# Five bf16 casts of the W_out combinations on GpSimd, with a re-annealed order of steps, in a fused cross-covariance attention and GELU MLP kernel

## The chip, the cores and the metric

The kernel runs on one core of one Trainium2 chip. The metric is the device time of one launch in microseconds (us); less is better. A core has five engines that work in parallel, each through its own instructions in order: TensorE (PE, matmuls from SBUF into PSUM), VectorE (DVE), ScalarE (ACT), GpSimd (POOL) and SyncE (SP, used here for DMAs). An engine that needs another's result waits for a semaphore. PSUM has eight banks, which this kernel hands out by name.

## What is computed

```python
qn = q / (norm(q, axis=1) + 1e-6)            # q, k, v: [4, 6080, 256]
kn = k / (norm(k, axis=1) + 1e-6)
a  = softmax(kn.transpose(0, 2, 1) @ qn / tau)   # [4, 256, 256]
x  = (v @ a).reshape(24320, 256)
h  = x @ w_in                                # [24320, 2048]
g  = 0.5 * h * (1 + tanh(sqrt(2/pi) * (h + 0.044715 * h**3)))
out = g @ w_out                              # [24320, 256]
```

Inputs and output are fp32; the kernel multiplies in bf16 with fp32 sums.

## The kernel before, in words

**The work.** For each of the four batches the kernel forms the 256x256 Gram matrix of K and Q and the squared norms, makes the softmax matrix `a` of them, and folds it into the first weight: `aw = a @ w_in`, 256x2048, in bf16. The MLP then is gelu(v @ aw) @ w_out. It goes over 25 blocks of tokens (mostly 1024; the 6080 tokens of a batch end in one of 960, the last batch in one of 448 and one of 512). Block n, half f of the hidden units and half t of the tokens give the activations `g`.

**Seven products in place of eight.** Both matmuls of a block are cut into 2x2 quarters and done as a Winograd form of Strassen's scheme: seven products m1 to m7 (first matmul) and M1 to M7 (second) instead of eight, at the price of sums. Sums of the V halves are made by `sums_v` (L568, step `vs`), of the aw halves by `sums_w` (L558, `SW`), of the activations by `token_sum` (L695, steps T1 to T4). The second matmul's other operand is eight combinations of the quarters of W_out, the tile `wcomb` (each 128 x 1024 bf16): A11, A12, A21, A22 are plain casts of a quarter, S1 to S4 are sums and differences. M1 reads A11, M2 A12, M3 S4, M4 A22, M5 S1, M6 S2, M7 S3; A21 is read only in the last block. In block 0 and in parts of block 1 the first matmul is done plainly (steps `g`, with `G` for the GELU).

**W_out's preparation** (L651 to L688). `load_wout` brings W_out as fp32 into `wst`, in two halves, through GpSimd's DMA queue. `prep_wout` has ten steps of one instruction each, all 128x1024: pA11 casts A11; pF0 makes wf0 = A21 - A22 in fp32, pS1 casts it to S1; pF1 makes wf1 = A11 - wf0, pS2 casts it to S2; pS4 and pS3 are differences that write bf16; pA12, pNA (A22) and pA21 cast quarters. `wst` shares its buffer with block 1's second half of `g`, so that half's GELUs can only write when all readers of `wst` are done. It happens once, in the first 65 us, beside block 0.

**What sets the order.** Nothing is scheduled by the compiler. The string `ORDER` (from L1008) lists 4030 steps; `run` (L918) takes them one by one and issues each step's instructions on their engines, so every engine's queue is in the order of this string. A word is `step.arguments@bank:block` (or `:batch`); `@f` names the PSUM bank. The string was annealed against a planner's costs. The steps that the text below names: `g`, `m1` to `m7`, `M1` to `M7`, `aw`, `vp` (V transposes on PE) and `row` (Gram rows) are PE's; `ac` (aw out of PSUM), `vc` (V out of PSUM), `SW`, `vs`, `T1` to `T4`, `ksq`/`qsq` (squares of K and Q; some on ACT) and `f1` to `f3` (their folds) are mostly VectorE's; `G`, `wG*`, `wcq`, `wy5`, `cq`, `y5` are ScalarE's.

**GpSimd's queue.** The steps `lq`, `lk` (`load_one`, L96) and `lv` (`cast_v`, L443) issue the DMAs of Q, K and V for later use, with a cast to bf16 under way. Each is made to wait for the matmul issued last before it (the `GATE`), so that loads are spread over time. T3 of blocks 1 to 22 is a DMA that accumulates (L709). All of these pass through GpSimd in order, one behind the other. Apart from them it does little: two fills and a `pow` of 128x4 per batch (L298).

Of the kernel before, what the change touches and what calls it, by code (L numbers as in the profile page):

```python
# [11 lines left out]
AF = mybir.ActivationFunctionType  # L12
# [4 lines left out]
def kernel(  # L17
# [648 lines left out]
    def prep_wout(what):  # L666
        if what == "pA11":
            nc.vector.tensor_copy(wc(A11), w_half(0, 0))
        if what == "pF0":
            WF.append(yout.tile([128, 32, 32], FP32, tag="ot", name="wf0"))  # L670
            nc.vector.tensor_sub(WF[0], w_half(1, 0), w_half(1, 1))
        if what == "pS1":
            nc.vector.tensor_copy(wc(S1), WF[0])
        if what == "pF1":
            WF.append(yout.tile([128, 32, 32], FP32, tag="ot", name="wf1"))
            nc.vector.tensor_sub(WF[1], w_half(0, 0), WF[0])
        if what == "pS4":
            nc.vector.tensor_sub(wc(S4), w_half(0, 1), WF[1])
        if what == "pS2":
            nc.vector.tensor_copy(wc(S2), WF[1])  # L680
        if what == "pA12":
            nc.scalar.activation(wc(A12), w_half(0, 1), AF.Copy)
        if what == "pNA":
            nc.scalar.activation(wc(A22), w_half(1, 1), AF.Copy)
        if what == "pA21":
            nc.scalar.activation(wc(A21), w_half(1, 0), AF.Copy)
        if what == "pS3":
            nc.vector.tensor_sub(wc(S3), w_half(1, 0), w_half(0, 0))  # L688
# [320 lines left out]
g.1_0@f:0 aw.2@g:0 g.0_0@e:0 aw.3@a:0 ac.2:0 g.2_0@b:0 ac.3:0 vp.1@z:0 G.0_0:0 g.6_0@c:0 aw.4@d:0  # L1009
vc.1_0:0 vc.1_1:0 g.4_0@g:0 aw.5@e:0 aw.7@a:0 ac.4:0 ac.5:0 ac.7:0 lk.0:1 SW.0:0 G.6_0:0 g.5_0@c:0  # L1010
pS3:0 g.5_1@d:0 aw.6@e:0 ac.6:0 G.2_0:0 G.1_0:0 lq.0:1 g.0_1@b:0 G.4_0:0 G.5_0:0 G.5_1:0 G.0_1:0
g.7_0@f:0 g.11_1@g:0 g.10_1@c:0 g.7_1@a:0 pA21:0 g.1_1@d:0 G.11_1:0 vp.0@z:1 g.8_0@b:0 pA11:0
G.7_1:0 G.7_0:0 G.1_1:0 G.10_1:0 g.12_0@g:0 SW.1:0 g.4_1@a:0 g.2_1@e:0 g.6_1@f:0 g.13_1@d:0 G.12_0:0
g.9_1@c:0 vc.0_0:1 pF0:0 lv.1:1 G.2_1:0 G.6_1:0 G.4_1:0 vc.0_1:1 G.13_1:0 g.11_0@g:0 g.15_0@e:0
g.10_0@f:0 g.3_0@a:0 g.3_1@d:0 G.11_0:0 g.0_0@g:1 G.8_0:0 G.15_0:0 G.3_0:0 lq.1:1 g.12_1@b:0 pF1:0
lt.1:1 pS1:0 pS2:0 T1.1:0 G.0_0:1 G.3_1:0 G.9_1:0 g.8_1@e:0 G.10_0:0 g.11_0@a:1 G.8_1:0 G.12_1:0
g.4_0@g:1 pS4:0 g.3_0@d:1 T1.0:0 ksq.0:1 qsq.0:1 g.13_0@c:0 g.9_0@f:0 g.15_1@e:0 g.14_1@b:0 G.4_0:1
G.9_0:0 G.3_0:1 G.14_1:0 G.15_1:0 g.14_0@g:0 row.0_2@z:1 G.13_0:0 lk.1:1 g.7_0@f:1 m1.1@d:1
row.0_4:1 row.0_0:1 M1.0@b:0 T2.1:0 f1.0:1 G.7_0:1 pNA:0 g.2_0@e:1 lk.2:1 pA12:0 M5.1@c:0 M5.0:0
wcq.1@f:1 G.2_0:1 G.11_0:1 G.14_0:0 M1.1:0 lv.0:2 g.8_0@e:1 G.8_0:1 row.0_3:1 y5:0 row.0_5:1 m2.1:1  # L1020
g.15_0@a:1 g.10_1@g:1 vs:1 lq.2:1 m5.1@e:1 g.10_0@c:1 wGp.1:1 G.15_0:1 wy5.1:1 f2.0:1 T2.0:0
g.15_1@f:1 m6.1:1 m5.6@a:1 g.11_1@e:1 G.10_0:1 f3.0:1 wap.1@c:1 row.0_1:1 T3.1:0 row.1_0:1 row.1_4:1
lv.1:2 G.15_1:1 G.11_1:1 G.10_1:1 m1.5@f:1 m7.1:1 g.2_1@e:1 m3.1:1 row.1_2:1 cq@g:0 row.1_1:1
row.1_3:1 row.1_5:1 wGs.1:1 wax.1:1 wy5.6:1 m5.5@c:1 m4.1:1 T4.1:0 gc:1 lq.3:1 M6.1:0 T3.0:0
sp.0@z:1 M6.0:0 M2.0:0 wy5.5:1 wGr.1:1 qsq.1:1 ksq.1:1 ap@a:0 M2.1:0 G.2_1:1 wcq.5@c:1 g.0_1@d:1
# [369 lines left out]
```

## Time and profile before

| | before |
|---|---|
| time, median of 3 runs | 677.4 us (677.34 to 677.78) |
| the profiled execution's own time | 677.52 us |
| its span, first to last instruction | 675.7 us |
| granted TensorE clock | 0.999 |
| DMA | 101.70 MB, mean 151 GB/s |

The profile's totals give each engine's busy time as a share of the span. The view of waits names, for each engine and line, whom it waited for, with the total, the number and the longest. The view by windows gives the busy time of the engines in each stretch, then the granted clock, the DMA share and GB/s. A timeline row is start, length, engine, line, operation and tiles; where several instructions are merged, the length runs from the first's start to the last's end, and `x` counts them. Lengths of neighbours on one engine overlap a little; the distance from start to start is what an instruction costs its engine.

### The profile page before, as it was taken

The numbers are of one execution on the slowest core, as the hardware profiler recorded it, in microseconds if no ns is written. First come the engines' busy times: TensorE is split into PE (matmuls) and PEld (weight loads), VectorE is DVE, ScalarE is ACT, GpSimd is POOL, SyncE is SP. The second block draws the span as 40 slices with busy tenths as digits, with TensorE's granted clock in tenths as the row PEclk, the third lists the DMA queues.
The fourth block names the chain that finished last, engine by engine and source line by source line (L and its number), as shares of the span: only waits on it lengthen the run. The fifth ranks groups of instructions, "written<-read, shape, count | busy, mean of one in ns | idle before, by whom it ended". The sixth has DMA issues, their size and how long they took to land.

```text
span 675.7 us, 10621 instructions
## 1 busy us (share of the span) xinstructions
PE 659.6 (98%) x3557; PEld 334.3 (49%) x3557; DVE 629.0 (93%) x977; ACT 624.4 (92%) x1201; POOL 113.1 (17%) x177
## 2 busy tenths in 40 slices
PE   3999999999999999999999999999999999999997
PEld 1854454554454454544444445445444444444567
DVE  3688999999999999999999999999999999999994
ACT  4389999999999999999999999999998999999984
POOL 4321121230211211102111111122011011011100
PEclk9999999999999999999999999999999999999999
DMA  9998899999879997868979999697484576457343
GB/s 241 208 263 134 145 171 172 180 154 168 158 153 182 168 178 128 167 103 150 148 147 169 186 149 191 103 172 147 101 156 98 117 152 140 80 122 154 63 95 107
DMA packets 167207, 101.70 MB, mean 151 GB/s; under 512 B 148128, under 2 KB 152352, under 8 KB 166432
## 3 DMA queue, kind: packets, MB, share of 16 engines
q0 software_dynamic: 20688, 62.34, 53.3%
q1 hardware_dynamic: 145264, 37.13, 26.3%
q10 hardware_dynamic: 1200, 1.56, 0.7%
q8 instruction: 28, 0.46, 0.3%
q14 instruction: 27, 0.22, 0.1%
HBM read 78.91 MB, written 36.57 MB: 171 GB/s over the span
## 4 chain that ended last, share of the span: by engine, by line
PE 94%; DMA 4%; DVE 1%; issue 0%; ACT 0%; POOL 0%; DVEq 0%; ACTq 0%; POOLq 0%
PE rb L491 20%; PE p L491 18%; PE q L491 16%; PE r L491 12%; PE m L491 11%; PE h L491 8%; PE G L205 5%; DMA qk_g1b<-in_k_dram 3%; PE awp L379 2%; DMA qk_g1a<-in_q_dram 1%; PE o L491 1%; PE ss L186 0%; PE ss L267 0%; PE rk L321 0%; DVE sq L160 0%
## 5 line engine op out<-in xcount | busy, mean ns | idle before, releaser
L491 PEld LDWEIGHTS <-wcomb 128*128 128x128 bf16 x1344 | 130.6, 98 | 144.6 <-issue 1.2
L641 ACT ACTIVATE g<-q 128x512 bf16<-128x512 f32 (+1 forms) x306 | 182.1, 621 | 4.4 <-PE q L491 3.8
L491 PE MATMUL rb<-tv,sw 128*128 128x512 bf16 (+3 forms) x334 | 117.0, 368 | 0.0
L632 DVE TENSOR_TENSOR q<-rb,yw 128x512 f32<-128x512 f32 (+2 forms) x160 | 108.6, 685 | 8.2 <-ACT g L549 2.3
L715 DVE TENSOR_TENSOR t<-g,t 128x2048 bf16<-128x2048 bf16 (+2 forms) x96 | 112.3, 1177 | 0.0
L635 DVE TENSOR_TENSOR xw<-rb,yw 128x512 f32<-128x512 f32 (+2 forms) x160 | 107.4, 675 | 3.8 <-PE rb L491 2.3
L491 PEld LDWEIGHTS <-aw 128*128 128x128 bf16 x757 | 73.4, 98 | 73.9 <-issue 1.0
L641 ACT ACTIVATE g<-xw 128x512 bf16<-128x512 f32 (+1 forms) x153 | 99.3, 652 | 1.2 <-DVE xw L635 1.2
L623 ACT ACTIVATE q<-rb 128x512 f32<-128x512 f32 (+2 forms) x160 | 96.8, 611 | 3.3 <-PE rb L491 1.7
L491 PEld LDWEIGHTS <-sw 128*128 128x128 bf16 x668 | 65.0, 98 | 64.4 <-issue 1.1
L641 ACT ACTIVATE g<-rb 128x512 bf16<-128x512 f32 (+1 forms) x153 | 93.5, 617 | 3.3 <-PE rb L491 3.0
L491 PE MATMUL r<-g,wcomb 128*128 128x512 bf16 (+2 forms) x384 | 95.1, 372 | 0.0
L491 PE MATMUL p<-t,wcomb 128*128 128x512 bf16 (+2 forms) x384 | 95.1, 372 | 0.0
L629 ACT ACTIVATE yw<-m 128x512 f32<-128x512 f32 (+2 forms) x145 | 89.8, 625 | 2.6 <-PE m L491 1.5
L549 ACT ACTIVATE g<-h 128x512 bf16<-128x512 f32 (+1 forms) x124 | 71.9, 647 | 3.8 <-PE h L491 3.7
L709 POOL DMA_DIRECT2D g<-g x44 | 39.5, 942 | 205.7 <-ACT g L641 109.8
L491 PE MATMUL h<-vT,aw 128*128 128x512 bf16 (+1 forms) x256 | 69.7, 378 | 0.3 <-DVE aw L421 0.3
L491 PE MATMUL q<-vT,sw 128*128 128x512 bf16 (+3 forms) x167 | 60.1, 368 | 0.0
L491 PE MATMUL q<-vT,aw 128*128 128x512 bf16 (+3 forms) x167 | 59.6, 368 | 0.0
L491 PE MATMUL rb<-vT,aw 128*128 128x512 bf16 (+3 forms) x167 | 59.4, 368 | 0.0
L491 PE MATMUL m<-tv,sw 128*128 128x512 bf16 (+3 forms) x167 | 59.3, 368 | 0.0
L491 PE MATMUL rb<-tv,aw 128*128 128x512 bf16 (+3 forms) x167 | 59.1, 368 | 0.0
(154 smaller groups left out, 876.3 us busy)
## 6 DMA issues: line engine op xcount, KB each, us to landing
out_dram<-ot SPq DMA_DIRECT2D x161, 128.0 KB, 3.4
g<-g POOLq DMA_DIRECT2D x38, 512.0 KB, 5.9
vb<-in_v_dram POOLq DMA_DIRECT2D x38, 256.0 KB, 5.1
k<-in_k_dram POOLq DMA_DIRECT2D x21, 384.0 KB, 6.3
q<-in_q_dram POOLq DMA_DIRECT2D x21, 384.0 KB, 6.7
g<-g POOLq DMA_DIRECT2D x6, 480.0 KB, 6.2
out_dram<-ot SPq DMA_DIRECT2D x24, 120.0 KB, 5.6
wst<-in_moe_w_out_dram POOLq DMA_DIRECT2D x2, 1024.0 KB, 10.0
```

The costliest lines, as they stand in the source:

```text
L205: nc.tensor.matmul(G[b][:, jc, :], lhsT=qt[:np_, r, jc * 128 : jc * 128 + 128], rhs=kt[:np_, r, :], start=first and jc == 0, stop=jc == 1, ...
L379: nc.tensor.matmul(ps, lhsT=ET[b][:, jc, ic * 128 : ic * 128 + 128], rhs=win_bf[:, jc, fs * 512 : fs * 512 + 512], start=jc == 0, stop=jc ...
L491: GATE[0] = nc.tensor.matmul(*a, skip_group_check=True, **kw)
L549: nc.scalar.activation(g_half(n, u // 8)[:, x, u % 8], hp[:, :hc], AF.Gelu_apprx_tanh)
L623: nc.scalar.activation(Q[n, i, 0][:, :w], RB[n, i][:, :w], AF.Copy)
L629: nc.scalar.activation(YW[n, i][:, :w], M5.pop((n, i))[:, :w], AF.Copy)
L632: nc.vector.tensor_add(Q[n, i, 1][:, :w], RB[n, i][:, :w], YW[n, i][:, :w])
L635: nc.vector.tensor_add(XW[n, i][:, :w], RB[n, i][:, :w], YW.pop((n, i))[:, :w])
L641: nc.scalar.activation(g[:, t, k0], x[:, :w], AF.Gelu_apprx_tanh)
L709: nc.gpsimd.dma_start(out=o, in_=quarter(n, 1, 1, h), accum_op=ALU.add)
L715: (nc.vector.tensor_add if add else nc.vector.tensor_sub)(o, a, b)
```

## The change

Five of the ten preparation steps move to GpSimd: S1 and S2 from VectorE, A12, A22 and A21 from ScalarE.

```diff
         if what == "pS1":
-            nc.vector.tensor_copy(wc(S1), WF[0])
+            nc.gpsimd.tensor_copy(wc(S1), WF[0])
...
         if what == "pS2":
-            nc.vector.tensor_copy(wc(S2), WF[1])
+            nc.gpsimd.tensor_copy(wc(S2), WF[1])
         if what == "pA12":
-            nc.scalar.activation(wc(A12), w_half(0, 1), AF.Copy)
+            nc.gpsimd.tensor_copy(wc(A12), w_half(0, 1))
         if what == "pNA":
-            nc.scalar.activation(wc(A22), w_half(1, 1), AF.Copy)
+            nc.gpsimd.tensor_copy(wc(A22), w_half(1, 1))
         if what == "pA21":
-            nc.scalar.activation(wc(A21), w_half(1, 0), AF.Copy)
+            nc.gpsimd.tensor_copy(wc(A21), w_half(1, 0))
```

`ORDER` holds the same 4030 words with the same arguments and blocks. Their places differ in five stretches, each followed by one where they are as before: the first 458 words, words 500 to 823, 1600 to 1798, 2503 to 2698 and 3100 to 3300 (by the old kernel's matmuls about 37 to 116 us, 122 to 170, 290 to 320, 430 to 460 and 522 to 556). Bank letters differ throughout. Part of the new string, from its 44th word on (the old one's order of the same steps can be read in the kernel above):

```
vp.0@z:1 g.4_1@f:0 g.9_1@c:0 lq.0:1 pA21:0 g.7_1@b:0 g.12_0@d:0 g.15_1@g:0 lv.1:1 G.4_1:0 G.9_1:0
G.11_0:0 G.7_1:0 g.10_1@f:0 g.13_1@c:0 G.15_1:0 G.12_0:0 g.8_1@a:0 vc.0_0:1 vc.0_1:1 pA11:0 pF0:0
pA12:0 lq.1:1 pF1:0 pS3:0 SW.1:0 G.13_1:0 pS4:0 G.8_1:0 G.6_1:0 T1.1:0 ksq.0:1 g.11_1@b:0 g.4_0@g:1
g.14_0@d:0 g.12_1@c:0 pNA:0 G.4_0:1 g.10_0@a:0 g.0_1@e:0 G.10_1:0 g.1_1@g:0 g.13_0@f:0 G.12_1:0
qsq.0:1 g.8_0@c:1 G.10_0:0 G.0_1:0 lt.1:1 g.15_0@a:0 g.10_0@e:1 G.14_0:0 G.11_1:0 G.15_0:0 f1.0:1
row.0_5@z:1 f2.0:1 row.0_2:1 g.9_0@d:0 g.2_0@b:1 g.15_0@a:1 row.0_4:1 lk.1:1 G.1_1:0 G.9_0:0 G.15_0:1
M1.1@g:0 g.14_1@d:0 G.2_0:1 G.13_0:0 T1.0:0 G.10_0:1 G.8_0:1 G.14_1:0 pS1:0 g.0_0@a:1 lv.0:2 T2.0:0
f3.0:1 g.7_0@b:1 M1.0:0 G.0_0:1 vs:1 g.3_0@f:1 m1.1@e:1 M5.1@c:0 lq.2:1
...
M5.0:0 row.0_1:1 m5.1@a:1 row.0_0:1 G.7_0:1 G.11_1:1 lv.1:2
...
T3.0:0 cq@c:0 pS2:0
...
```

More of the change, by code (lines that the diff above doesn't have):

```diff
@@ L1008 @@
 ORDER = """
[L1009 to L1025, printed above, removed]
@@ new lines @@
+g.7_0@d:0 g.5_0@e:0 aw.5@b:0 aw.4@c:0 G.7_0:0 G.3_0:0 G.0_0:0 g.6_0@d:0 vc.1_0:0 vc.1_1:0 g.3_1@a:0
+g.2_1@g:0 G.5_0:0 G.6_0:0 G.2_1:0 G.3_1:0 G.1_0:0 aw.6@e:0 g.5_1@d:0 ac.5:0 ac.4:0 ac.6:0 g.8_0@b:0
+g.4_0@c:0 G.4_0:0 SW.0:0 aw.7@g:0 g.11_0@a:0 ac.7:0 g.6_1@e:0 G.8_0:0 G.5_1:0 vp.0@z:1 g.4_1@f:0
+g.9_1@c:0 lq.0:1 pA21:0 g.7_1@b:0 g.12_0@d:0 g.15_1@g:0 lv.1:1 G.4_1:0 G.9_1:0 G.11_0:0 G.7_1:0
+g.10_1@f:0 g.13_1@c:0 G.15_1:0 G.12_0:0 g.8_1@a:0 vc.0_0:1 vc.0_1:1 pA11:0 pF0:0 pA12:0 lq.1:1 pF1:0
+pS3:0 SW.1:0 G.13_1:0 pS4:0 G.8_1:0 G.6_1:0 T1.1:0 ksq.0:1 g.11_1@b:0 g.4_0@g:1 g.14_0@d:0
@@ new lines @@
+g.12_1@c:0 pNA:0 G.4_0:1 g.10_0@a:0 g.0_1@e:0 G.10_1:0 g.1_1@g:0 g.13_0@f:0 G.12_1:0 qsq.0:1
+g.8_0@c:1 G.10_0:0 G.0_1:0 lt.1:1 g.15_0@a:0 g.10_0@e:1 G.14_0:0 G.11_1:0 G.15_0:0 f1.0:1
+row.0_5@z:1 f2.0:1 row.0_2:1 g.9_0@d:0 g.2_0@b:1 g.15_0@a:1 row.0_4:1 lk.1:1 G.1_1:0 G.9_0:0
+G.15_0:1 M1.1@g:0 g.14_1@d:0 G.2_0:1 G.13_0:0 T1.0:0 G.10_0:1 G.8_0:1 G.14_1:0 pS1:0 g.0_0@a:1
+lv.0:2 T2.0:0 f3.0:1 g.7_0@b:1 M1.0:0 G.0_0:1 vs:1 g.3_0@f:1 m1.1@e:1 M5.1@c:0 lq.2:1 G.3_0:1
+wcq.1@d:1 g.10_1@a:1 G.10_1:1 m2.1:1 g.11_1@f:1 M5.0:0 row.0_1:1 m5.1@a:1 row.0_0:1 G.7_0:1 G.11_1:1
@@ new lines @@
+lv.1:2 m6.1:1 y5:0 m1.5@b:1 T3.1:0 m5.5@f:1 row.0_3:1 wy5.1:1 wGp.1:1 T3.0:0 cq@c:0 pS2:0 row.1_0:1
+row.1_1:1 row.1_5:1 row.1_3:1 wap.1@a:1 lk.2:1 T2.1:0 row.1_2:1 row.1_4:1 wcq.5@d:1 wy5.5:1 M2.0:0
+gc:1 m2.5:1 m3.1:1 m7.1:1 sp.0@z:1 wGp.5:1 wGs.1:1 ksq.1:1 wax.1:1 qsq.1:1 g.15_1@f:1 m6.5:1 M6.1:0
+M2.1:0 g.11_0@d:1 wap.5@a:1 lt.1:2 f1.1:1 c11:0 f2.1:1 m3.5:1 m7.5:1 M6.0:0 G.11_0:1 G.15_1:1
+wGx.1:1 lt.0:2 g.2_1@d:1 g.0_1@g:1 lq.3:1 G.2_1:1 m4.1:1 sa.0:1 ap@f:0 wax.5:1 M3.1:0 G.0_1:1 f3.1:1
+m5.6@d:1 m1.6@g:1 m4.5:1 sp.1@z:1 M7.1:0 wGx.5:1 lk.3:1 wGr.1:1 wcq.6@e:1 wy5.6:1 T4.1:0 T4.0:0
@@ new lines @@
+c11:2 wGs.3:3 wGx.2:3 m2.4:3 row.4_0:1 m5.4@b:3 m7.3:3 m6.4:3 m1.5@e:3 c22:1 wGp.4:3 ksq.6:1 wax.3:3
+m5.5@a:3 M6.0:2 wy5.4:3 wGr.2:3 wcq.5@b:3 wap.4@d:3 row.4_1:1 wy5.5:3 m4.3:3 m6.5:3 m3.4:3 wGx.3:3
+row.4_2:1 row.4_3:1 m2.5:3 m7.4:3 wGr.3:3 f1.6:1 wGp.5:3 wap.5@a:3 row.5_4:1 wax.4:3 row.5_0:1
+wGs.4:3 m5.6@f:3 f2.6:1 ap@b:2 wGx.4:3 row.4_4:1 m7.5:3 row.5_3:1 row.5_5:1 m4.4:3 wy5.6:3 wGr.4:3
+f3.6:1 m1.6@d:3 m3.5:3 M3.1:2 lt.0:4 wcq.6@f:3 gc:1 sp.6@z:1 wGs.5:3 m5.7@g:3 wax.5:3 sa.6:1 qsq.7:1
@@ new lines @@
+m2.6:3 m6.6:3 ksq.7:1 M7.0:2 M7.1:2 wGp.6:3 wGx.5:3 wap.6@a:3 m3.6:3 lt.1:4 f1.7:1 ax:2 lv.0:5
+m1.7@f:3 m4.5:3 m7.6:3 wGs.6:3 M3.0:2 wcq.7@a:3 m6.7:3 lq.0:2 M4.1:2 wax.6:3 f2.7:1 wy5.7:3
+wap.7@g:3 f3.7:1 m4.6:3 m3.7:3 m2.7:3 m7.7:3 wGx.6:3 wGr.5:3 wGs.7:3 g.8_0@e:3 sp.7@z:1 c12:2
+wax.7:3 sa.7:1 T1.0:3 wGp.7:3 g.0_0@b:4 m1.3@g:4 wGr.6:3 lk.0:2 m4.7:3 G.8_0:3 M4.0:2 row.7_0@z:1
+m1.1@a:4 row.7_1:1 wGr.7:3 wcq.3@d:4 m2.3:4 row.6_4:1 g.0_1@e:4 vs:4 G.0_0:4 wcq.1@f:4 T3.0:3 m6.3:4
+m5.1@b:4 m2.1:4 pow:1 lv.1:5 row.6_5:1 row.7_2:1 m6.1:4 wGp.3:4 wGx.7:3 wy5.1:4 T1.1:3 c21:2
@@ new lines @@
+G.0_1:6 m3.5:6 wax.5:6 m6.6:6 wap.6@c:6 wGs.5:6 m1.4@d:6 M6.0:5 wcq.4@g:6 wGx.5:6 m4.5:6 m3.6:6
+m7.6:6 row.0_0:2 m5.7@b:6 row.1_5:2 T4.0:5 wGs.6:6 wGr.5:6 wax.6:6 m2.4:6 row.0_2:2 wy5.7:6 m5.4@c:6
+m6.4:6 lk.4:2 ap@f:5 m4.6:6 wy5.4:6 m1.7@b:6 wGp.4:6 wcq.7@c:6 lv.0:9 M3.1:5 wGr.6:6 M3.0:5 m6.7:6
+gc:2 T4.1:5 wGx.6:6 wap.4@g:6 m2.7:6 m3.4:6 m7.4:6 wGp.7:6 M7.0:5 wap.7@e:6 wax.4:6 m7.7:6 wGx.4:6
+m3.7:6 m4.4:6 wGr.4:6 wGs.4:6 c12:5 M7.1:5 m1.4@c:7 wGs.7:6 wax.7:6 m4.7:6 g.8_0@f:7 ax:5 g.8_1@d:7
@@ new lines @@
+G.8_1:12 T1.1:11 m1.4@e:12 m4.3:12 wGx.3:12 row.1_2:3 wGs.1:12 wGr.3:12 wcq.4@c:12 wax.1:12
+M5.0@a:11 SW.1:2 T3.1:11 M5.1:11 m1.2@b:12 m2.4:12 wGx.1:12 y5:11 wGp.4:12 row.1_1:3 T2.1:11
+row.1_5:3 wcq.2@d:12 m4.1:12 m6.4:12 m5.4@a:12 M1.1@c:11 wy5.4:12 wy5.2:12 wGr.1:12 m2.2:12 T2.0:11
+lq.2:3 lk.2:3 m6.2:12 M1.0:11 m1.5@a:12 wap.4@g:12 m3.4:12 wap.2@f:12 m7.4:12 row.0_4:3 m3.2:12
+m7.2:12 wGp.2:12 ksq.1:3 cq@d:11 wax.4:12 wGs.4:12 wcq.5@g:12 M2.1:11 T4.1:11 wGs.2:12 wGx.4:12
+m2.5:12 m4.4:12 wGr.4:12 wGp.5:12 m6.5:12 m5.5@f:12 M2.0:11 wax.2:12 c22:10 wy5.5:12 m1.6@e:12
```

643 lines of the change are left out of this document (310 added, 333 removed).

## The prediction, made before the changed kernel was run

> **What bounds the kernel now.** I read the page's totals first, then the list of what TensorE waits for, then stretches of 10 us, then the chain of waits, and last the timelines of VectorE and GpSimd around W_out's preparation.
>
> ```profile
> span 675.7 us, 10621 instructions
> PE 659.6 (98%) x3557; PEld 334.3 (49%) x3557; DVE 629.0 (93%) x977; ACT 624.4 (92%) x1201; POOL 113.1 (17%) x177
> ...
> PE G L205 <- ACT qk_g1a L131: 10.2, 2, 7.2
> PE ss L261 <- DVE a L243: 1.3, 1, 1.3
> PE h L491 <- DVE aw L421: 0.3, 1, 0.3
> PE q L491 <- DVE q L815: 0.2, 1, 0.2
> ...
> 40.00:50.00 10.00, 10.00 (x59) 4.97 (x57) 9.58 (x19) 8.88 (x17) 1.09 (x2) 1.00 1.11 312
> 50.00:60.00 10.00, 10.00 (x51) 4.81 (x50) 10.00 (x12) 10.00 (x21) 1.94 (x4) 1.00 0.76 120
> 60.00:70.00 10.00, 10.00 (x60) 5.37 (x58) 7.59 (x12) 9.97 (x20) 2.31 (x5) 1.00 0.92 151
> ...
> 46.84 9.93 PE h L491 x46
> ```
>
> TensorE (PE) is the bound: 98% of the span. The waits that it lists are four lines, 12.0 us together; three of them belong to the head (no Q and K yet, no weights yet), and only the last, 0.2 us, comes after the head. A busy PE could still hide gaps, since one matmul's record overlaps the next. The chain's row at 46.84 shows that there are none there: 46 matmuls of 512 columns in 9.93 us are 0.216 us each, start to start, without a break. Taking every start-to-start interval above that pitch, from the first matmul of the plain steps to the last of the kernel,
>
> ```profile
> 37.53 0.65 PE L491 MATMUL h<-vT,aw 128*128 128x512 bf16 x2 [0.31 <-DVE aw L421]
> ...
> 668.65 3.22 PE L491 MATMUL o<-wcomb,g 128*128 128x256 bf16 x28
> ```
>
> I find about 2.3 us of gaps in all, of which 0.2 lie before 116 us (where W_out is prepared) and about 0.7 in the three later stretches whose steps the change reorders. So there is next to nothing to win: 0.9 us if every gap in the reordered stretches went. There is much to lose, since each us that PE waits is a us of the kernel. The windows from 40 to 60 us say who could make it wait: VectorE (DVE) and ScalarE (ACT) are both at 8.9 to 10.0 of 10.
>
> **The change part by part.** In the built program both versions give PE the same 3554 matmuls with the same 1,532,204 columns, in another order. PE's work therefore is unchanged; only waits can differ. Removed from the two busy engines:
>
> ```profile
> 44.77 1.05 ACT L686 ACTIVATE wcomb<-wst 128x1024 bf16<-128x1024 f32 x1
> 45.72 13.32 ACT L549 ACTIVATE g<-h 128x512 bf16<-128x512 f32 x27
> 58.70 1.26 ACT L684 ACTIVATE wcomb<-wst 128x1024 bf16<-128x1024 f32 x1
> 59.65 1.25 ACT L682 ACTIVATE wcomb<-wst 128x1024 bf16<-128x1024 f32 x1
> ...
> 50.57 1.21 DVE L676 TENSOR_TENSOR wf<-wst,wf 128x1024 f32<-128x1024 f32 x1
> 51.70 0.68 DVE L673 CAST wcomb<-wf 128x1024 bf16<-128x1024 f32 x1
> 52.30 0.68 DVE L680 CAST wcomb<-wf 128x1024 bf16<-128x1024 f32 x1
> 52.90 1.21 DVE L715 TENSOR_TENSOR t<-g 128x2048 bf16<-128x2048 bf16 x1
> 54.04 1.21 DVE L678 TENSOR_TENSOR wcomb<-wst,wf 128x1024 bf16<-128x1024 f32 x1
> 55.17 1.21 DVE L715 TENSOR_TENSOR t<-g 128x2048 bf16<-128x2048 bf16 x1
> 56.31 0.95 DVE L160 TENSOR_TENSOR sq<-k 128x1536 bf16<-128x1536 bf16 x1
> 57.18 0.95 DVE L160 TENSOR_TENSOR sq<-q 128x1536 bf16<-128x1536 bf16 x1
> 58.09 1.23 DVE L715 TENSOR_TENSOR t<-g,t 128x2048 bf16<-128x2048 bf16 x1
> ```
>
> ACT loses 0.95 us each by start-to-start (58.70 to 59.65), 2.85 us in all; VectorE 2 x 0.60 (51.70, 52.30, 52.90), 1.2 us. That relief itself is worth 0, because PE is not waiting there; its worth is only that the new order may call for results sooner.
>
> Added to GpSimd (POOL): five casts, 128x1024 fp32 to bf16. No row shows such a cast on it. The nearest are
>
> ```profile
> 0.24 0.10 POOL L1376 MEMSET const-float32-0.0<- 128x1 f32 x1 [0.24 <-issue]
> 4.65 0.27 POOL masks.py:197 MEMSET ident<- 128x128 f32 x1
> 4.99 0.29 POOL masks.py:199 TENSOR_SCALAR_AFFINE_SELECT ident<-ident 128x128 f32<-128x128 f32 x1
> ```
>
> The same cast on ScalarE, 1.05 us (at 44.77), is my lower end. GpSimd's own slope from 1 to 128 elements is 0.17 us for 127, which over 1024 gives 0.10 + 1.37, about 1.45 us: the upper one. I take the middle, 1.25. The Trainium skill (GPSIMD Engine Reference, section Elementwise — side-by-side cycle accounting) gives 1.8 cycles of 1.2 GHz an element as the best loop; by that estimate a cast is 1.54 us and each term below grows by a quarter. No run here shows it yet.
>
> GpSimd also issues the DMAs of Q, K and V, in order, each held back until a given matmul. A step's time in the new order I get by adding the columns of the matmuls ahead of it at 0.216 us per 512, from 37.5 us (for the old order this puts the first M5 at 59.1). An issue takes 0.53 to 0.55 us and follows its matmul by 0.3 to 0.5:
>
> ```profile
> 43.67 0.53 POOL L103 DMA_DIRECT2D q<-in_q_dram  x1 [1.17 <-PE h L491]
> 50.16 0.53 POOL L447 DMA_DIRECT2D vb<-in_v_dram  x1 [5.95 <-PE h L491]
> ...
> DMA to landing us min/median/max: 4.5/5.0/8.1
> ```
>
> The new queue is then: q1_0 at 48.4, pA21 at 48.9, vb1_1 at 50.2, pA12 at 50.7, q1_1 at 52.0, pNA at 52.5, k1_1 at 57.6, pS1 at 58.1, and later pS2 at 65.2. Three consumers could be late. q1_0 (issued at 43.67 before) lands at 53.4 by the median, at 56.5 at worst; the first gram row wants it at 55.5: cost 0, up to 1.0. S1 is ready at 59.4 for M5.1 at 61.0, S2 at 66.5 for M6.1 at 68.7, A12 and A22 long before use: cost 0. A21 is used in the last block only.
>
> VectorE is where it bites. In the new order its run from the second V transpose (47.3) to block 1's sums_v is, by the pitches above and these two rows,
>
> ```profile
> 60.10 0.68 DVE L573 TENSOR_TENSOR tv<-vT 128x1024 bf16<-128x1024 bf16 x1
> ...
> 61.62 0.42 DVE L181 TENSOR_TENSOR sq<-sq 128x512 bf16<-128x512 bf16 x1
> ```
>
> two copies of about a fold's 0.35 and pA11 at 0.60 (ends 48.7), pF0, pF1, pS3 (52.2), four sums of SW.1 (53.6), pS4, T1.1 (55.9), four squares and folds (58.9), T1.0 (60.1), T2.0, one fold, and sums_v at 1.5 (60.10 to 61.62), which ends at 63.2. m5.1 of block 1 reads sums_v's result at 63.9. So the margin is 0.7 us; T1.0 has 3 us before M5.0 at 62.9. T2.0 and a fold, 1.5 us, now run ahead of sums_v though M6 needs them only at 72.
>
> Does a cast on GpSimd slow VectorE? The trace has one GpSimd instruction that reads SBUF beside VectorE's work, three times:
>
> ```profile
> 138.25 1.65 POOL L298 TENSOR_TENSOR rt<-sv,halves 128x4 f32<-128x4 f32 x1
> 138.34 0.64 DVE L573 TENSOR_TENSOR tv<-vT 128x1024 bf16<-128x1024 bf16 x1
> 309.61 0.68 DVE L635 TENSOR_TENSOR xw<-rb,yw 128x512 f32<-128x512 f32 x1
> 309.78 1.05 POOL L298 TENSOR_TENSOR rt<-sv,halves 128x4 f32<-128x4 f32 x1
> 460.00 1.22 DVE L715 TENSOR_TENSOR t<-g 128x2048 bf16<-128x2048 bf16 x1
> 460.07 2.05 POOL L298 TENSOR_TENSOR rt<-sv,halves 128x4 f32<-128x4 f32 x1
> ```
>
> Beside an instruction with one operand in PSUM (xw) it took 1.05 us; beside one with both inputs in SBUF it took 0.60 longer (that instruction: 0.64) and 1.00 longer (of 1.22). The two engines share something, and GpSimd waited for it. These rows read four elements, so they can't show how long VectorE waits for a 1024-element read. Nearly all of the run from pF0 to sums_v has both inputs in SBUF, so four casts (pA21, pA12, pNA, pS1) meet it. What each takes from VectorE lies between nothing (it gives way, as the rows show) and its whole length. I take half of 1.25, halfway, since no row is nearer to either end: 4 x 0.62 = 2.5 us, less the margin of 0.7: **PE waits 1.8 us at m5.1**. pS2's place is followed by margins of about 1.6: 0. The gaps in the reordered stretches may give 0.2 back.
>
> The sum is +1.6 on the profiled execution's 677.52 (span 675.7 and 1.8 around it); that run lies 0.1 above the median of 677.4, so 679.0.
>
> The Trainium skill (SBUF — State Buffer, section Who interferes with whom) says that VectorE's second pair of ports is GpSimd's only one, that an instruction with two SBUF inputs contends with a GpSimd instruction that reads SBUF, and that whoever comes first holds it to its end. The rt rows agree for GpSimd's waits (0.60 and 1.00); for VectorE's no row does.
>
> **The rivals.**
> *Held for the whole cast.* Four whole casts at 1.05 to 1.45 are 4.2 to 5.8 us, less 0.7: 3.5 to 5.1, so 680.7 to 682.3. For it: VectorE's 10.00 of 10 in the window from 50 on. Against it: a cast that starts where VectorE works from PSUM holds nothing. The State Buffer page of the Trainium skill, above, would have it go this way.
> *GpSimd gives way.* VectorE loses under 0.2 us a cast, the sum stays below the margin of 0.7, and the order's shaved gaps leave 677.2, at most 0.2 us under the median. It decides from a loss of 0.7/4, about 0.2, a cast. For it: in both shared rt rows VectorE's instruction kept its length. This is the case on the other side, not slower.
> *GpSimd starves.* If it gives way to an unbroken run, pS1 comes after 61.0, and PE waits at M5.1 for S1, with the later issues behind it. A wait of one T (1.1) at each of two casts stays inside pS1's room of 1.6 only barely: 678 to 681.
> *Every gap goes.* 677.4 - 0.9 = 676.5; over 0.2% faster (below 676.05) would need gaps outside the reordered stretches too. That the casts don't move is excluded: the built program has all five on GpSimd.
>
> **How the numbers follow.** Held for a part (678.2 to 680.0) 0.36, held whole 0.24, gives way 0.32, starves 0.04, gaps go 0.04. A measurement can tell about 0.2%, 1.35 us, from no change: below 676.05 and above 678.75. Slower: 0.24 + 0.25 of the first case + 0.03 = 0.52; faster 0.03, as the last case mostly stays within; same 0.45. The range from 676.8 to 682.0 leaves out the longest holds and the best of the gaps. The cases that are not slower have their own range, 676.6 to 678.2.
>
> **What would show it.** A row PE m <- DVE tv, or a gap at m5.1 near 64 us, of 1 to 2 us; SBUF-with-SBUF instructions of VectorE between 48 and 64 us longer than 1.23, or spaced wider than 1.14; casts of 1.0 to 2.5 us on GpSimd. If VectorE's rows keep their pitch, the sum is wrong at the hold; if PE waits for wcomb, GpSimd starved; if a gap stands past 120 us, the new order did it and not the casts.

## The result, and the profile after

The changed kernel takes **682.26 us** (median of 20 runs, 681.91 to 682.77), the kernel before 677.77 (20 runs beside them, 677.34 to 683.36). The ratio is 1.0059, 95% interval 1.0049 to 1.0069: slower by 3.3 to 4.7 us. Here and below the ratios are not those of the medians: single executions some us above the rest (before: 680.59 and 683.36) move them, so both are given. The prediction was 679.0, in a range from 676.8 to 682.0; the time lies 0.3 above its upper end and 0.04 inside the rival "held for the whole cast" (680.7 to 682.3). But the kernel before took 0.4 us more here than the 677.4 that the prediction starts from: 677.4 times the ratio is 681.4, inside the range, near its upper end and in the middle of that rival.

The profiled execution after took 682.38 us with a span of 680.6 (before: 677.52 and 675.7). These are its totals, what TensorE waited for after the head, and the two windows from 50 to 70 us (columns as before):

```profile
span 680.6 us, 10605 instructions
PE 661.4 (97%) x3557; PEld 334.4 (49%) x3557; DVE 634.8 (93%) x975; ACT 623.6 (92%) x1198; POOL 120.5 (18%) x182
...
PE h L491 <- ACT g L549: 2.3, 1, 2.3
PE m L491 <- DVE tv L573: 1.0, 1, 1.0
PE q L491 <- DVE q L632: 0.8, 1, 0.8
...
50.00:60.00 10.00, 8.92 (x45) 4.21 (x43) 9.93 (x8) 7.36 (x16) 4.82 (x7) 1.00 0.89 141
60.00:70.00 10.00, 7.83 (x40) 3.76 (x40) 9.83 (x14) 8.18 (x17) 2.29 (x4) 1.00 0.59 98
```

Three waits are new: TensorE waits 2.3 us for a GELU, 1.0 us for block 1's `sums_v` (the place that the prediction named) and 0.8 us for a sum at L632. From 50 to 70 us its busy time falls from 20.00 to 16.75, while VectorE is as good as full (19.76). Counted as in the prediction (start-to-start intervals over the pitch of 0.216 us for 512 columns, records that are missing from the trace left out), TensorE's gaps between 37 and 116 us are 5.25 us where they were 0.24; after 116 us they are 2.3 where they were 2.0. So nearly the whole loss stands beside the preparation of W_out, and the later stretches of the new order gave nothing. Here is why VectorE is late. First GpSimd's timeline of the changed kernel, then VectorE's and ScalarE's:

```profile
48.63 0.53 POOL L103 DMA_DIRECT2D q<-in_q_dram  x1 [7.39 <-PE h L491]
49.16 1.05 POOL L686 CAST wcomb<-wst 128x1024 bf16<-128x1024 f32 x1
50.15 0.53 POOL L447 DMA_DIRECT2D vb<-in_v_dram  x1
50.67 1.05 POOL L682 CAST wcomb<-wst 128x1024 bf16<-128x1024 f32 x1
51.65 0.55 POOL L103 DMA_DIRECT2D q<-in_q_dram  x1
52.20 1.05 POOL L684 CAST wcomb<-wst 128x1024 bf16<-128x1024 f32 x1
57.71 0.53 POOL L103 DMA_DIRECT2D k<-in_k_dram  x1 [4.46 <-PE h L491]
58.23 1.05 POOL L673 CAST wcomb<-wf 128x1024 bf16<-128x1024 f32 x1
...
69.27 1.71 POOL L680 CAST wcomb<-wf 128x1024 bf16<-128x1024 f32 x1
```

```profile
48.78 5.55 DVE L671 TENSOR_TENSOR wf<-wst 128x1024 f32<-128x1024 f32 x1
...
58.11 2.26 DVE L678 TENSOR_TENSOR wcomb<-wst,wf 128x1024 bf16<-128x1024 f32 x1
...
67.34 0.68 DVE L573 TENSOR_TENSOR tv<-vT 128x1024 bf16<-128x1024 bf16 x1
...
68.86 3.19 DVE L715 TENSOR_TENSOR g<-g,g 128x2048 bf16<-128x2048 bf16 x2
71.97 0.69 DVE L632 TENSOR_TENSOR q<-rb,yw 128x512 f32<-128x512 f32 x1
```

```profile
60.53 4.03 ACT L549 ACTIVATE g<-h 128x512 bf16<-128x512 f32 x8 [3.17 <-DVE wcomb L678]
```

The row to read first is pF0 at 48.78: one subtraction of 5.55 us, where it took 1.21. It began 0.38 us *before* the first cast and ended at 54.33, which is 1.08 us after the third cast's end (53.25): about the length of a subtraction. So it did next to nothing through three casts and the two DMA issues between them. pS4 at 58.11 took 2.26 beside S1's cast (+1.05), and the pair of T3 sums at 68.86 took 3.19 beside S2's, where such a pair takes 2.35 (+0.84). VectorE loses 4.34 + 1.05 + 0.84 = 6.2 us.

The lateness shows first where the prediction did not look. `wst` shares its buffer with block 1's second half of `g`; pS4 (L678) is its last reader, and ScalarE's GELU at 60.53 has waited 3.17 us for it. TensorE runs on until no PSUM bank is free and then stands still for 2.42 us from 58.76, 1.12 us from 66.96 (m5.1, for `sums_v`) and 0.93 us from 71.79 (L632).

### The profile page after: what moved, and what is told of

The parts are those of the page before. It is cut to its first block, busy times and chain, and to the rows that moved or that the text cites. A ratio compares the mean times of both kernels' runs of the same rounds, so it can differ in the third digit from the quotient of the medians.

```text
span 680.6 us, 10605 instructions
## 1 busy us (share of the span) xinstructions
PE 661.4 (97%) x3557; PEld 334.4 (49%) x3557; DVE 634.8 (93%) x975; ACT 623.6 (92%) x1198; POOL 120.5 (18%) x182
## 4 chain that ended last, share of the span: by engine, by line
PE 87%; DVE 5%; DMA 4%; ACT 2%; issue 1%; POOL 1%; DVEq 0%; POOLq 0%; ACTq 0%
PE rb L491 19%; PE p L491 17%; PE q L491 15%; PE r L491 11%; PE m L491 10%; PE h L491 6%; PE G L205 4%; DMA qk_g1b<-in_k_dram 3%; PE awp L379 2%; DMA qk_g1a<-in_q_dram 1%; ACT g L641 1%; DVE wf L671 1%; DVE t L715 1%; DMA out_dram<-ot 1%; PE o L491 1%
## 5 line engine op out<-in xcount | busy, mean ns | idle before, releaser
L632 DVE TENSOR_TENSOR q<-rb,yw 128x512 f32<-128x512 f32 (+2 forms) x160 | 108.7, 686 | 5.1 <-PE rb L491 1.1
```

The lines of the kernel that those rows point to most:

```text
L632: nc.vector.tensor_add(Q[n, i, 1][:, :w], RB[n, i][:, :w], YW[n, i][:, :w])
```

## The experiments

The theory behind the first four: the casts' hold on VectorE is the whole loss. The rivals: the new order of steps does it, or ScalarE's share. Each run is compared with the kernel before on the same chip; its median there was 677.51 us for e1 to e4, 677.34 for e5 to e7 and 677.59 for e8. "VectorE held" is what VectorE's instructions between 42 and 72 us took over their usual length, "TensorE's gaps" are those from 37 to 116 us; both are us of the profiled execution.

| kernel | time, us | ratio to before, 95% interval | VectorE held | TensorE's gaps |
|---|---|---|---|---|
| before | 677.77 | | 0 | 0.24 |
| changed | 682.26 | 1.0059 (1.0049 to 1.0069) | 6.2 | 5.25 |
| e1 new order, casts as before | 679.93 | 1.0035 (1.0023 to 1.0048) | 0 | 2.33 |
| e2 old order, casts on GpSimd | 677.91 | 1.0019 (0.9999 to 1.0039) | 4.7 | 1.32 |
| e3 new order, two casts | 679.16 | 1.0030 (1.0019 to 1.0040) | 1.1 | 2.33 |
| e4 new order, three casts | 683.60 | 1.0084 (1.0068 to 1.0099) | 4.2 | 4.47 |
| e5 pS4 earlier | 682.44 | 1.0077 (1.0062 to 1.0092) | 6.4 | 5.58 |
| e6 `sums_v` earlier too | 682.69 | 1.0080 (1.0065 to 1.0095) | 6.4 | 5.47 |
| e7 issues taken out from between | 680.76 | 1.0051 (1.0034 to 1.0068) | 5.1 | 4.11 |
| e8 each cast waits for the last | 680.77 | 1.0046 (1.0029 to 1.0063) | 4.6 | 3.52 |

**e1_order_only: the order alone.** The changed kernel with all five casts back on VectorE and ScalarE.

```diff
-            nc.gpsimd.tensor_copy(wc(S1), WF[0])
+            nc.vector.tensor_copy(wc(S1), WF[0])
...
-            nc.gpsimd.tensor_copy(wc(A12), w_half(0, 1))
+            nc.scalar.activation(wc(A12), w_half(0, 1), AF.Copy)
```

> The new order of steps with all five casts back on VectorE and ScalarE. If the casts on GpSimd cost the time (they stop VectorE: its first subtraction took 5.55 us in place of 1.21), nearly all of the loss of 4.5 us goes: 677.0 to 678.2, no gap of over 0.3 us on PE between 40 and 75 us, the subtraction at 1.21. If the new order costs it (margins annealed too thin), 681 or more, with the gaps at the same steps as in the changed kernel.

Measured: 679.93 us, above what was expected and below what the rival would have. VectorE's subtractions are at 1.22 again and between 40 and 116 us TensorE waits for none of its results, but 1.6 us are gone elsewhere. These are rows of this kernel's list of waits and of ScalarE's timeline:

```profile
PE h L491 <- ACT g L549: 1.3, 2, 0.8
...
51.06 1.13 ACT L682 ACTIVATE wcomb<-wst 128x1024 bf16<-128x1024 f32 x1
...
53.44 1.16 ACT L684 ACTIVATE wcomb<-wst 128x1024 bf16<-128x1024 f32 x1
```

Two casts on ScalarE now stand among GELUs for which TensorE waits (gaps of 0.64 and 1.00 behind the matmuls at 51.9 and 53.9). The new order has no room for them there. So my "relief worth 0" holds in the old order only; in the new one ScalarE's relief is worth 1.6 us of gaps.

**e2_casts_only: the casts alone.** The kernel before, its order untouched, with the five casts on GpSimd (the edits of the change without its string).

> The old order of steps with the five casts on GpSimd. If the casts stop VectorE, it loses up to 5 x 1.05 us here and gains 1.2; the old order left about 3 us of room before sums_v is wanted, so PE waits 1 to 2 us: 678.5 to 680, and the VectorE instructions beside a cast are longer by 1.05 each. If the new order is the cause, 677.2 to 678.0.

Measured: 677.91 us, the median of ten executions from 677.73 to 683.75. That is less than the theory gave and inside the range that was set for "the new order is the cause"; the interval, from no change to 0.4% slower, leaves it open whether the casts cost anything in this order. What speaks against that rival is the trace: VectorE is held for 4.7 us here too, as its timeline shows:

```profile
53.34 3.33 DVE L678 TENSOR_TENSOR wcomb<-wst,wf 128x1024 bf16<-128x1024 f32 x1
...
57.72 1.99 DVE L160 TENSOR_TENSOR sq<-k 128x1536 bf16<-128x1536 bf16 x1
...
60.50 2.07 DVE L715 TENSOR_TENSOR t<-g,t 128x2048 bf16<-128x2048 bf16 x1
```

pS4 waits out two casts back to back (3.33 in place of 1.21), a square and a sum one each, and a short sum of SW ahead of this run waits out most of pA21's (0.72). Yet TensorE loses only 1.32 us in gaps: the old order has the slack behind these instructions. Of the hold, four fifths become gaps in the new order (5.0 of 6.2) and a quarter in the old one (1.1 of 4.7). So the theory that the hold is the whole loss does not stand as it was put: by the medians the order alone costs 2.4 us (e1) and the casts alone 0.4, while both together cost 4.5. The hold costs what it does because the new order leaves no slack behind the held instructions.

**e3_two_casts and e4_three_casts: which casts.** e3 keeps S1 and S2 on GpSimd and puts the three quarters back on ScalarE; e4 keeps the three quarters on GpSimd and puts S1 and S2 back on VectorE, both in the new order.

```diff
-            nc.gpsimd.tensor_copy(wc(A12), w_half(0, 1))
+            nc.scalar.activation(wc(A12), w_half(0, 1), AF.Copy)
```

> The changed kernel with A12, A22 and A21 back on ScalarE, so that only S1 and S2 are cast on GpSimd. If the casts stop VectorE: the first subtraction is back at 1.21, one later VectorE instruction is longer by 1.05 (beside S1) and T3 by 0.8 (beside S2), ScalarE waits no more for VectorE before it overwrites W_out's buffer; 677.4 to 678.8. If the order is the cause, 681 or more. If the loads behind the casts in GpSimd's queue are the cause, about half of the loss stays: 679 to 681.

```diff
-            nc.gpsimd.tensor_copy(wc(S1), WF[0])
+            nc.vector.tensor_copy(wc(S1), WF[0])
```

> The changed kernel with S1 and S2 back on VectorE, so that A12, A22 and A21 are cast on GpSimd. If the casts stop VectorE, the first subtraction stays at 5.5 us, since all three of these fall on it; VectorE has 1.2 us more of its own and 1.9 us less of waits: 680.5 to 682. If the cost is per cast and the same for each, three fifths of the loss: 680.0. If the order is the cause, as the changed kernel, 682.

e3: 679.16 us, with the two gaps of e1 to a hundredth (0.64, 0.99) and VectorE held for 1.1 us only: the miss has e1's cause. S1 and S2 on GpSimd cost nothing that these times show.

e4: 683.6 us, above what was expected. pF0 takes 4.64, pF1 beside the third cast 1.94; and S1's cast, which stands behind T1.0 in this order, comes too late on a VectorE that has been held. Rows of e4's waits, of its GpSimd timeline and of its windows:

```profile
PE m L491 <- DVE wcomb L673: 2.7, 1, 2.7
```

```profile
51.28 0.55 POOL L103 DMA_DIRECT2D q<-in_q_dram  x1
51.83 2.11 POOL L684 CAST wcomb<-wst 128x1024 bf16<-128x1024 f32 x1
```

```profile
62.00:66.00 4.00, 1.27 (x6) 0.55 (x6) 3.96 (x6) 1.44 (x3) 0.00 (x0) 0.97 0.07 13
66.00:70.00 4.00, 4.00 (x14) 1.63 (x13) 3.93 (x6) 2.10 (x4) 0.55 (x1) 0.60 0.60 96
```

Here the third cast waited 1.06 us: GpSimd does yield, after two. And the wait for S1 costs twice: the window behind it has a granted clock of 0.60 (the seventh column), so that 1.6 us of its 4.00 are lost although TensorE is busy throughout, which the gaps do not count. The Trainium skill (TensorE: Matmul & The Clock Gate, section What's actually happening) says that the clock falls to a half after an idle window of some 3.4 us. The run agrees with the fall to a half (from 65.76 to 69 us matmuls of 512 columns start every 0.43 us in place of 0.216), but not with the idle time: TensorE had stood still for only 2.7 us.

So the three quarters, cast in one run beside pF0, are the larger part of the hold (4.34 of 6.2 us). The second question is where it is felt.

**e5_early_release and e6_vs_first: is it the buffer, or VectorE's lateness?** e5 moves pS4, the last reader of `wst`, up by five instructions of VectorE; e6 besides puts T2.0 and a fold behind `sums_v`.

```diff
-pS3:0 SW.1:0 G.13_1:0 pS4:0 G.8_1:0 ...
+pS4:0 pS3:0 SW.1:0 G.13_1:0 G.8_1:0 ...
```

> The changed kernel with pS4 right behind pF1 and SW.1 behind pS3, so that VectorE is done with W_out's buffer 2.5 us earlier, with the same work in all. Theory: VectorE is late by what the casts hold it, and ScalarE's 3.2 us wait for that buffer is only where this shows first. Then PE's 2.4 us gap at 58.6 goes and the one at m5.1 grows by about as much: 681.5 to 682.5. Rival: the wait for the buffer is a cause by itself; then 2 us come back: 679.8 to 680.5.

```diff
-lv.0:2 T2.0:0 f3.0:1 g.7_0@b:1 M1.0:0 G.0_0:1 vs:1 ...
+lv.0:2 g.7_0@b:1 M1.0:0 G.0_0:1 vs:1 T2.0:0 f3.0:1 ...
```

> The former, and T2.0 and the fold f3 behind sums_v, which takes 1.5 us of work that is not urgent from in front of sums_v. If VectorE's lateness at sums_v sets PE's wait, the gap at m5.1 shrinks by 1.5 us against the former: 680.0 to 681.2. If something else holds PE there, no change against the former.

e5: 682.44 us, as the theory had it. ScalarE's wait before these GELUs is down from 3.17 to 0.80 us and TensorE's gap of 2.42 is gone, and TensorE waits instead for T1.1 and T1.0 (gaps 0.76 and 2.29), then as before for `sums_v` and L632. e6: 682.69, a miss. The gap at m5.1 is gone, and the one at L632 has grown from 0.93 to 1.94. What TensorE loses is VectorE's lateness at the end of an unbroken run from 47 to 72 us; which step shows it is a matter of the order. The prediction's remark that T2.0 runs needlessly ahead of `sums_v` was true and worth nothing.

**p1_probe: the contention by itself.**

> Leaves out the whole computation: only VectorE instructions of one form at a time, with casts of 1024 fp32 to bf16 on GpSimd (the quarter's strided form) or DMA issues beside them, and some tile written out. If GpSimd's cast takes precedence over a VectorE instruction with two SBUF inputs: ten fp32 subtractions (11.4 us alone) take 14.5 us beside three casts, the casts keep 1.05 us each. If whoever started first holds the port to its end: each cast lengthens by the rest of the running VectorE instruction (0 to 1.1 us), and the sum on VectorE is the same 3.2 us. For bf16 sums of 2048 the second is what the changed kernel's last cast showed (1.71 us). Beside PSUM operands and beside nothing: casts at 1.05, VectorE unchanged. Three DMA issues alone lengthen VectorE by nothing; with casts between them, the subtraction in the changed kernel lost 4.4 us to three casts and two issues, so 4.2 us if the issues count too and 3.2 if they don't.

The rows are VectorE's timeline: nine of ten subtractions alone, nine of ten beside three casts (the first of ten has a row of its own), then fifteen sums with one operand in PSUM beside three casts.

```profile
123.19 10.30 DVE L59 TENSOR_TENSOR o<-a,b 128x1024 f32<-128x1024 f32 x9
...
14.11 12.82 DVE L59 TENSOR_TENSOR o<-a,b 128x1024 f32<-128x1024 f32 x9
...
68.11 9.05 DVE L67 TENSOR_TENSOR o<-p,a 128x512 f32<-128x512 f32 x15
```

Three casts cost nine subtractions 2.5 us, 0.84 each: casts and subtractions take turns, a cast then takes about 2.0 us from start to end. fp32 to bf16 and bf16 sums cost the same to 0.01. VectorE's own fp32 casts from SBUF lose too (11.63 us for 15, where 15 at their pitch of 0.60 are 9.0). With an operand in PSUM there is no loss (0.60 each, and the casts at their 1.05). So a cast costs VectorE most of itself, but this alternation does not make a subtraction of 5.55. DMA issues alone cost nothing (nine subtractions take 10.30 beside three). With issues between the casts eleven subtractions lost 2.9 us, but there each later issue waited for the landing of the one before, so that this was no run without a break.

**e7_casts_together: the issues between the casts.** Two words of the string move, so that q1_0's and v1_1's DMA issues stand ahead of the three casts and q1_1's behind them.

```diff
-lq.0:1 pA21:0 ... lv.1:1 ... pA12:0 lq.1:1 ... pNA:0
+lq.0:1 ... lv.1:1 pA21:0 ... pA12:0 ... pNA:0 lq.1:1
```

> The changed kernel with the two DMA issues taken out from between the three quarters' casts on GpSimd (vb1_1 ahead of them, q1_1 behind them). If a run of casts and issues without a break holds VectorE until its end, the first subtraction is now passed by between casts and VectorE loses 3.1 us there and not 4.4: 680.8 to 681.6. If each cast simply costs its length, 3.1 us were lost either way and the issues counted for nothing: 682.0 to 682.6, subtractions longer by 1.05 each or one of them by 3.1.

Measured: 680.76 us. Rows of its GpSimd and VectorE timelines:

```profile
49.55 0.53 POOL L447 DMA_DIRECT2D vb<-in_v_dram  x1 [0.76 <-PE h L491]
50.06 1.05 POOL L686 CAST wcomb<-wst 128x1024 bf16<-128x1024 f32 x1
51.05 1.04 POOL L682 CAST wcomb<-wst 128x1024 bf16<-128x1024 f32 x1
52.03 1.04 POOL L684 CAST wcomb<-wst 128x1024 bf16<-128x1024 f32 x1
```

```profile
48.40 1.22 DVE L671 TENSOR_TENSOR wf<-wst 128x1024 f32<-128x1024 f32 x1
49.66 4.50 DVE L676 TENSOR_TENSOR wf<-wst,wf 128x1024 f32<-128x1024 f32 x1
```

The time is at the lower end of what was expected, the way to it is another: still one subtraction waits out all three casts, without any issue between them. Of the hold, the two issues' 1.05 us went. A DMA issue between two casts is time in which the waiting subtraction gets no turn either.

**p2_probe, e8_casts_chained, p3_probe: what makes the long hold.** p2 tries issues and casts in turn with three kinds of VectorE instruction and three starts.

> Leaves out the whole computation, as the first probe: eight VectorE instructions of one form (fp32 in one run, fp32 in runs of 32 as W_out's halves, bf16), with issue, cast, issue, cast, issue, cast on GpSimd without a break, in three phases against each other; then with three casts alone, three issues alone, nothing. If GpSimd keeps the port across an issue between two casts, one subtraction is 4 us or longer in at least one phase, and with three casts alone none is over 2.3. If only runs of 32 lose, only that form does. If neither shows, what held the first subtraction in the changed kernel for 4.4 us stays open; each cast then costs about 1.0 in every form.

No subtraction took over 2.34 us. There all casts write one tile, so each waits for the one before it; in the kernel they are independent. e8 is the changed kernel with that one difference:

```diff
+    def cast_pool(o, i):
+        inst = nc.gpsimd.tensor_copy(o, i)
+        after(inst, CAST[-1] if CAST else None)
+        CAST.append(inst)
...
-            nc.gpsimd.tensor_copy(wc(A12), w_half(0, 1))
+            cast_pool(wc(A12), w_half(0, 1))
```

> The changed kernel, order and engines as they are; each of GpSimd's five casts waits, besides what it reads, for the cast before it. Theory (independent casts follow one another so closely that a VectorE instruction that waits for the shared way into SBUF gets no turn; a cast that waits for the one before it lets one VectorE instruction through): pF0 takes at most 2.3 us in place of 5.55, the subtraction finishes between two casts, VectorE loses about 1.05 per cast, and the kernel is 1.0 to 1.3 us faster than the changed one, 680.8 to 681.5. Rival (VectorE gets no turn for another reason: GpSimd's DMA issues between the casts, or how long its own instruction has waited): pF0 is still 5.5 us and the time 682.0 to 682.6.

Measured: 680.77 us. VectorE's timeline of e8, with GpSimd's last two of the three casts (its helper gives all casts one line, and moves the other lines by 6):

```profile
48.51 2.52 DVE L677 TENSOR_TENSOR wf<-wst 128x1024 f32<-128x1024 f32 x1
51.06 1.94 DVE L682 TENSOR_TENSOR wf<-wst,wf 128x1024 f32<-128x1024 f32 x1
52.93 2.05 DVE L694 TENSOR_TENSOR wcomb<-wst 128x1024 bf16<-128x1024 f32 x1
```

```profile
50.39 1.54 POOL L668 CAST wcomb<-wst 128x1024 bf16<-128x1024 f32 x1
...
52.42 1.48 POOL L668 CAST wcomb<-wst 128x1024 bf16<-128x1024 f32 x1
```

pF0 is through after one cast, and from there the two engines take turns, nearly as the theory had it (at most 2.3 us for pF0). By the medians the added waits make the kernel 1.5 us faster: the changed one's 20 executions lie between 681.91 and 682.77 us, e8's four, of a later round, between 680.33 and 680.85. The intervals of the two ratios overlap, so the gain itself is likely and not shown. p3 then tries independent and chained casts by themselves.

> It leaves out the whole computation and only times VectorE instructions beside GpSimd's work: eight contiguous fp32 subtractions, eight fp32 subtractions over runs of 32, or eight bf16 sums, behind a short copy, beside (a) a DMA issue and a cast in turn, three times, the casts writing three tiles, (b) three casts writing three tiles, (c) three casts writing the same tile, so that each waits for the one before it. Theory (a run of independent casts keeps VectorE's instruction waiting through all of them): in (a) and (b) one VectorE instruction of 4 to 5.5 us and the others at their usual 1.2; in (c) three of about 2.05. Rival (it is the kernel's layout or its DMA traffic, not the dependence of the casts): (a), (b) and (c) all show instructions of at most 2.3 us. If only (a) shows the long one, the DMA issues between do it.

The theory held in part. Casts back to back take turns with subtractions whether they depend on each other or not. A long one came with issues between independent casts, and only behind one of the two starts, with the same 4.20 us for all three kinds; this is the fp32 one, VectorE's row and GpSimd's:

```profile
46.00 4.20 DVE L66 TENSOR_TENSOR o<-a,b 128x1024 f32<-128x1024 f32 x1
```

```profile
45.47 0.74 POOL L85 DMA_DIRECT2D land<-in_k_dram  x1 [0.27 <-issue]
46.21 1.05 POOL L78 CAST y<-x 128x1024 bf16<-128x1024 f32 x1
47.19 0.53 POOL L85 DMA_DIRECT2D land<-in_k_dram  x1
47.71 1.05 POOL L78 CAST y<-x 128x1024 bf16<-128x1024 f32 x1
```

p2 has the same start (0.54 us into the issue) with chained casts: 2.34 us. So with independent casts the hold is long, but something else must start it. p4 asked whether it is the lead over the cast.

> It leaves out the whole computation and only times six contiguous fp32 subtractions of VectorE beside three casts of GpSimd (fp32 to bf16, to three tiles, so that none waits for another), back to back or with a DMA issue between each two; fillers of 128x1 move the first subtraction from about 0.4 us behind the first cast's start to about 1 us ahead of it, in eight steps. In the changed kernel and in two of its variants the subtraction began 0.38 to 0.41 us before the cast, and was held through two or three casts. Theory (what decides is the lead of the subtraction's start over the first cast's): with a lead over about 0.6 us the first subtraction takes 1.2 us and the cast waits for it, then they take turns (2.05 each); with a lead of 0 to about 0.4 the subtraction does nothing before the second or third cast's end, 4 to 5.5 us; behind the cast, about 2.05 to 2.3, and turns. Rival (the lead does not matter; what the rest of the kernel does at that time does): no subtraction over 2.4 us at any lead. If long ones come only with the DMA issues between, these keep it waiting.

Lead alone does not do it: a subtraction 0.19 us ahead of three casts went first, at its usual 1.21. The one long row of p4 (3.03 us) came in the variant with issues, from a start in the middle of one; these are VectorE's row and GpSimd's:

```profile
20.01 3.03 DVE L79 TENSOR_TENSOR o<-a,b 128x1024 f32<-128x1024 f32 x1
```

```profile
19.76 0.66 POOL L71 DMA_DIRECT2D land<-in_k_dram  x1
20.42 1.05 POOL L67 CAST y<-x 128x1024 bf16<-128x1024 f32 x1
```

That is the pattern of all runs. I took every VectorE instruction with two SBUF inputs that began while GpSimd issued a DMA with a cast next in its queue. Of those that began 0.11 to 0.55 us after the issue's start, 23 of 24 were held, by 1.0 to 4.3 us (the exception is a short sum of 0.42 us in e2, before a cast that starts 0.10 us after its issue has ended); the 7 that began within 0.10 us of it kept their length. Without a cast behind the issue nothing is held: none of over 90 such starts in the kernel before and the changed one. That goes for the `pow` of L298 too, which reads SBUF: in the kernel before, the sum at 460.00 began 0.45 us into the issue ahead of it and kept its 1.22 us. So a cast that stands behind a DMA issue takes its turn, as VectorE sees it, about 0.1 us after that issue's start, not at its own. With chained casts the hold ends after one; with independent ones it could go on. I read this from the runs after they were made; none was made to test it. Why GpSimd keeps its turn over an issue of 0.53 us, why `pow` does not take one so early, and why the hold ended after one cast in p4, after two in e4 and p3 and after three in the changed kernel and e7, stays open.

## Why the prediction was right in direction and off in size

- **TensorE is the bound, and its work is unchanged.** Right: 3557 matmul records before and after, and the loss is in waits. The 4.9 us between the profiled executions agree with the 5.0 us of new gaps.
- **What the casts hit.** Right: VectorE's instructions with two SBUF inputs, and not those with one in PSUM. Right too that S1, S2, A12, A22 and q1_0 come in time. The 0.2 us that the later stretches might have given back did not come.
- **"I take half of 1.25": this term was mis-sized.** It is why 1.6 us were forecast where the ratio gives 4.0. The cast is 1.05 us, the lower end, and not 1.25. But it holds VectorE for 0.84 to 1.06 us, four fifths of it or all, never half; and three of the four are not separate holds: pF0 stands through all three and the two issues between, 4.34 us. The four that I put at 2.5 us took 5.4. The Trainium skill (SBUF — State Buffer, section Who interferes with whom) has the whole length of the one that comes first, which is the right size for one cast; by the start times in the timeline pF0 came first, by 0.38 us, and lost. Counting the DMA issue in front of the cast as GpSimd's coming would mend that, and no run here shows what the issue itself holds.
- **"pS2's place ... 0"**: 0.84 us on the T3 pair, right ahead of the sum at L632 for which TensorE waits 0.8 us. The margin of 1.6 had been used up by then.
- **Where it shows.** m5.1 waits 1.12 us (I had 1.8), but it is the second place. I followed the products that wait for VectorE's *results* and left out the buffer that `pS4` *releases*; ScalarE stands 3.17 us behind it, and TensorE 2.42 us behind ScalarE. e5 shows that this cost nothing by itself: without it as much is lost at T1.1 and T1.0.
- **"Relief worth 0."** Wrong for the new order: without it, e1 loses 1.6 us in ScalarE's place. The change therefore is the sum of a gain that its own order makes necessary and a hold that this order has no room for.
- **The rivals.** "Held for the whole cast" gave the time; I had 0.24 for it. That is in part luck: its four separate casts at 1.05 would have been 4.2 us, and the 5.4 that were measured hold the two DMA issues besides, which it left out. "Gives way" read three rows in which GpSimd waited for VectorE, but those instructions read 4 elements, and they differ from the casts in more than length (each stood behind a DMA issue, and the sum at 460.00 was not held): they could not show the other direction, which the prediction says and then still gave 0.32.

The old order with the casts moved (e2) is the best of the variants, and it does not beat the kernel before. No variant could do so by much: TensorE's gaps there were only 0.24 us before.

## What to carry to other kernels

Work moved to an idle GpSimd is not free when it reads SBUF beside VectorE's two-input instructions: price each cast at its whole length on VectorE, a run of independent casts as one hold with the DMA issues between them, and look at which VectorE instruction will start while GpSimd issues the DMA ahead of it. Put such casts where VectorE reads PSUM, or let each wait for the one before it (e8). Where the bound engine has no gaps, a hold of a helper engine costs what the order's slack behind it leaves, so by the medians the same five casts cost 0.4 us in one order (e2) and 2.3 in the other (the changed kernel over e1), where they also freed 1.6; follow the buffers that a late instruction releases as well as its results.

## What the runs showed of the hardware that I had not expected

- GpSimd casts 128x1024 from fp32 to bf16 in 1.05 us, the same as ScalarE's 1.05; where it waits for a VectorE instruction, the same cast shows up to 2.1 us. The estimate of 1.54 from the Trainium skill (GPSIMD Engine Reference, section Elementwise — side-by-side cycle accounting) is not borne out; the same section has 1.03 cycles for short loops that the ports bound, by estimate 0.88 us, and the measured cast lies between the two.
- A subtraction that the trace shows as running for 5.55 us was waiting for 4.3 of them: a shared way into SBUF shows as a longer instruction, not as idle time, so no view of waits names it.
- With waits added between GpSimd's casts (e8) the span of the profiled execution was 678.9 us, where the changed kernel's was 680.6.
- One wait of TensorE of 2.7 us in e4 was followed by about 4 us at a granted clock of 0.60.
